# A long convolution beside attention: product stationary and Toeplitz rows streaming in four column tiles, in place of Toeplitz tiles stationary and product streaming

## The chip, the cores and the metric

One core of one Trainium2 chip runs the whole program. The time is microseconds of device time for one execution, and the median of several executions is quoted. All comparisons are between fast runs, and where a single execution is all there is, that is said.

Engines are named as in the profile: PE is the matmul array, PEld its weight loads, DVE the vector engine, ACT the activation engine, POOL and SP the two others. SP does nothing here but issue DMA.

## The reference, cut to what matters

Two independent halves are joined along the last axis. Half A is attention with 32 heads of 16 over 2048 tokens. Half B is a causal convolution of length 2048, one kernel for each of 512 channels. Written as a matrix product, a channel's kernel becomes a Toeplitz matrix: each row is the row above, shifted by one token.

```python
def _A_ref(x, wqkv, wo):                 # x: 1 x 2048 x 512, bf16
    qkv = (x @ wqkv).reshape(B, S, 3, H, Dh)...     # H = 32, Dh = 16
    p = softmax(einsum("bhqd,bhkd->bhqk", q, k) * Dh ** -0.5)
    return einsum("bhqk,bhkd->bhqd", p, v)... @ wo

def _B_ref(q, k, v, shift_k, ssm_k, ssm_D):
    k_shift = sum of k shifted by 0..3 tokens, each times shift_k[:, j]
    kv = k_shift * v                     # the "product", 2048 x 512
    y = causal convolution of kv with ssm_k along the tokens (done there by FFT)
    return q * (y + kv * ssm_D)
```

The attention needs one exp for each of 32 x 2048 x 2048 scores. In this program that is ACT's work alone.

## The kernel before

The program is one long loop of 694 steps. Step T issues up to three score matmuls (row tiles of 32), one exp over what they wrote (128 x 1536), up to three matmuls of an earlier step's probabilities with the values ("PV", column tiles of 32), and one piece of background work on PE: a projection, or one channel of the convolution.

```python
def emit_qk(T): ...      # 3 matmuls, lhsT = KTo[32*s:32*s+32, ...], N = 512, tile_position=(32*s, 0)
                         # then ACT: PT[:, T % R_PT, ...] = exp(SCALE * PS[...])
def emit_pv(bl, T): ...  # 3 matmuls, N = 512, tile_position=(0, 32*s), all into bank PVB

def load_wr(d):          # 128 overlapping rows of channel d's kernel: row p is the kernel shifted by p
    src = bass.AP(tensor=kz_ap.tensor, offset=kz_ap[d, 1].offset, ap=[[1, 128], [1, S]])   # 512 KB
    h_wr[d] = dma(sp, d_wr[r], WR[:, r, :], src, deps)

def conv_chan(d):        # one channel, one step: 16 lags of 128 tokens
    for n in range(NB):                                              # NB = 16
        ins = e.matmul(PS[:, BGB, NB * c + n:NB * c + NB],
                       lhsT=WR[:, r, 128 * n:128 * n + 128],         # Toeplitz tile is stationary
                       rhs=KV[:, 0:NB - n, d], start=(n == 0), stop=(n == NB - 1))  # 16 to 1 columns
    ...                  # after 32 channels DVE multiplies the bank by q
```

The program divides PSUM into eight banks: six alternate between the scores of two steps, one takes PV, one takes the background work (BGB). The exp of step T must be done before the scores of step T+2 may overwrite its banks, so ACT and PE run two steps apart at most.

The softmax here doesn't subtract the row's maximum and nothing guards it: scores larger than these inputs give would overflow.

## Time and profile before

| what | value |
|---|---|
| time | 1153.4 us (1152.6 to 1158.3, 4 runs) |
| profiled execution, span | 1151.7 us |
| start, until the convolution begins | 144 us, 68 steps |
| convolution beside attention | 901 us |
| attention alone, then the end | 90 us + 17 us |

The first view is the page's chart of 40 equal slices, in tenths: how busy PE, ACT and the DMA engines were, and the PE clock that was granted (9 is 90% or more of full speed).

```profile
...
PE   7968999999999999999999999999999999999887
...
ACT  3745898989898989898988898989899889889995
...
PEclk8966855555557565656665656665555575655556
DMA  8742788889997979897989697979999969890000
...
```

PE looks full, ACT is at 80 to 90%, and the DMA engines are at 9 or so in most slices. PEclk: 5 or 6 for nearly the whole convolution stage. PE is "99% busy" (895 of 901 us) at a mean clock of 0.57, mostly 0.50.

Next the costliest groups. After the bar stand busy us and mean ns of one, after the second bar the idle time before them and what ended it.

```profile
...
L387 ACT ACTIVATE PT<-PS 128x1536 bf16<-128x1536 f32 (+1 forms) x694 | 974.4, 1466 | 158.3 <-PE PS L380 156.6
...
L517 PEld LDWEIGHTS PS<-KV,WR 128*128 128x128 bf16 x8192 | 257.5, 103 | 216.4 <-issue 216.4
L517 PE MATMUL PS<-KV,WR 128*128 128x16 bf16 (+15 forms) x8192 | 299.5, 177 | 2.7 <-DVE QT L266 1.8
...
```

ACT waited 157 us for score matmuls, the largest wait that it has; most of it lies between two exps of the convolution stage. PE's convolution shows as 258 us of 128-column weight loads beside matmuls that stream 16 columns or fewer.

The stretches view gives busy time by engine (with the number of instructions), granted clock, DMA share and GB/s for the stage with convolution and for the attention alone after it (an instruction cut by the edge of a stretch counts):

```profile
...
core 0: us, PE busy (x) PEld busy (x) DVE busy (x) ACT busy (x) POOL busy (x), PEclk, DMA share, GB/s
144.00:1045.00 901.00, 894.72 (x11713) 391.96 (x11709) 177.65 (x257) 799.89 (x558) 10.44 (x16) 0.57 0.88 299
1045.00:1135.00 90.00, 78.13 (x407) 14.53 (x404) 16.52 (x24) 90.00 (x68) 0.78 (x1) 0.50 0.03 6
...
```

In the first stage 558 exps fall in 901 us, one in 1.61 us, at a mean clock of 0.57. In the second 68 fall in 90 us, one in 1.33 us, and ACT is busy all the time. So 1.33 us a step is ACT's own floor, and the convolution costs 0.28 us a step above it.

One step of the convolution stage on PE, from the timeline (start, us to the end of the group, what):

```profile
...
602.38 0.62 PE L409 MATMUL PS<-PT,VAF 128*32 128x512 bf16 x3
602.93 0.58 PE L517 MATMUL PS<-KV,WR 128*128 128x16 bf16 x16
603.45 0.61 PE L380 MATMUL PS<-QT,KTo 32*128 32x512 bf16 x3
603.99 0.62 PE L409 MATMUL PS<-PT,VAF 128*32 128x512 bf16 x3
```

Scores to scores takes 1.61 us: scores to PV 0.54, PV to convolution 0.55, convolution 0.52. The convolution's 16 pairs of weight load and matmul follow each other every 27 ns, although no matmul streams more than 16 columns.

### The profile page before, as it was taken

The numbers are of one execution on the slowest core, as the hardware profiler recorded it, in microseconds if no ns is written. First come the engines' busy times: TensorE is split into PE (matmuls) and PEld (weight loads), VectorE is DVE, ScalarE is ACT, GpSimd is POOL, SyncE is SP. The second block draws the span as 40 slices with busy tenths as digits, with TensorE's granted clock in tenths as the row PEclk, the third lists the DMA queues.
The fourth block names the chain that finished last, engine by engine and source line by source line (L and its number), as shares of the span: only waits on it lengthen the run. The fifth ranks groups of instructions, "written<-read, shape, count | busy, mean of one in ns | idle before, by whom it ended". The sixth has DMA issues, their size and how long they took to land.

```text
span 1151.7 us, 27251 instructions
## 1 busy us (share of the span) xinstructions
PE 1102.0 (96%) x12700; PEld 442.1 (38%) x12700; DVE 302.2 (26%) x445; ACT 977.1 (85%) x698; POOL 41.0 (4%) x52
## 2 busy tenths in 40 slices
PE   7968999999999999999999999999999999999887
PEld 2212244444443444444444343444444444442111
DVE  4898412111212011212101212211212111212112
ACT  3745898989898989898988898989899889889995
POOL 4000500000000000000000000000000000000000
PEclk8966855555557565656665656665555575655556
DMA  8742788889997979897989697979999969890000
GB/s 177 257 136 92 237 290 297 291 296 326 323 327 241 331 257 324 272 337 262 334 282 331 224 330 261 329 267 331 339 329 335 326 210 337 292 310 19 1 1 19
DMA packets 98735, 296.03 MB, mean 257 GB/s; under 512 B 18500, under 2 KB 30782, under 8 KB 98494
## 3 DMA queue, kind: packets, MB, share of 16 engines
q1 hardware_dynamic: 94574, 286.16, 74.3%
q0 software_dynamic: 2176, 6.29, 1.9%
q8 instruction: 99, 1.62, 0.6%
q10 hardware_dynamic: 1872, 1.84, 0.6%
q14 instruction: 14, 0.11, 0.0%
HBM read 285.73 MB, written 6.42 MB: 254 GB/s over the span
## 4 chain that ended last, share of the span: by engine, by line
PE 79%; ACT 12%; DVE 7%; DMA 1%; SPq 1%; issue 0%; DVEq 0%
PE PS L409 24%; PE PS L380 24%; PE PS L517 22%; ACT PT L387 12%; PE PS L233 3%; PE PS L472 3%; DVE QT L266 1%; PE PS L252 1%; PE PS L240 1%; DVE OUTA L480 1%; SPq L143 1%; DVE QN L302 1%; DVE DN L432 1%; DMA QN<-in_B_v_dram 1%; DMA xT<-in_A_x_dram 1%; DVE QN L306 1%
## 5 line engine op out<-in xcount | busy, mean ns | idle before, releaser
L387 ACT ACTIVATE PT<-PS 128x1536 bf16<-128x1536 f32 (+1 forms) x694 | 974.4, 1466 | 158.3 <-PE PS L380 156.6
L380 PE MATMUL PS<-QT,KTo 32*128 32x512 bf16 x2048 | 393.2, 561 | 15.9 <-ACT PT L387 13.5
L409 PE MATMUL PS<-PT,VAF 128*32 128x512 bf16 x2048 | 400.6, 567 | 0.0
L517 PEld LDWEIGHTS PS<-KV,WR 128*128 128x128 bf16 x8192 | 257.5, 103 | 216.4 <-issue 216.4
L517 PE MATMUL PS<-KV,WR 128*128 128x16 bf16 (+15 forms) x8192 | 299.5, 177 | 2.7 <-DVE QT L266 1.8
L409 PEld LDWEIGHTS PS<-PT,VAF 128*32 128x32 bf16 x2048 | 74.0, 100 | 273.1 <-issue 261.9
L424 DVE COPY OF<-PS 128x512 f32<-128x512 f32 x32 | 22.1, 692 | 543.1 <-PE PS L409 543.1
L380 PEld LDWEIGHTS PS<-QT,KTo 32*128 32x128 bf16 x2048 | 72.9, 98 | 115.0 <-ACT PT L387 75.2
L432 DVE RECIPROCAL DN<-DN 128x128 f32<-128x128 f32 x128 | 110.7, 916 | 0.9
L528 DVE TENSOR_TENSOR QN<-PS,QN 128x512 bf16<-128x512 f32 x16 | 11.1, 692 | 206.2 <-PE PS L517 206.2
L233 PE MATMUL PS<-xT,WQP 128*128 128x512 bf16 x128 | 43.4, 474 | 6.4 <-DMA xT<-in_A_x_dram 4.7
L472 PE MATMUL PS<-WKV,OTN 128*128 128x512 bf16 x128 | 41.8, 465 | 3.5 <-DVE OTN L437 2.3
L266 DVE CAST QT<-PS 128x512 bf16<-128x512 f32 x32 | 22.1, 691 | 33.4 <-PE PS L233 33.4
L426 DVE STREAM_SHUFFLE DN<-OF 128x512 f32<-128x512 f32 x32 | 24.1, 754 | 0.0
L143 POOL DMA_DIRECT2D out_dram<-QN x4 | 4.7, 1173 | 539.2 <-DVE QN L528 539.2
L437 DVE TENSOR_TENSOR OTN<-OF,DN 128x512 bf16<-128x512 f32 (+1 forms) x35 | 22.6, 646 | 1.2
L233 PEld LDWEIGHTS PS<-xT,WQP 128*128 128x128 bf16 x128 | 11.4, 110 | 29.7 <-issue 9.1
L472 PEld LDWEIGHTS PS<-WKV,OTN 128*128 128x128 bf16 x128 | 12.1, 111 | 27.2 <-issue 13.2
L240 PE MATMUL PS<-xT,WKV 128*128 128x512 bf16 x64 | 20.9, 459 | 0.9 <-DVE KTo L270 0.9
L252 PE MATMUL PS<-WKV,xT 128*128 128x512 bf16 x64 | 18.3, 413 | 2.7 <-DVE VAF L280 2.7
L245 PE MATMUL PS<-KV,JEX 128*128 128x512 bf16 x16 | 7.9, 491 | 13.0 <-DVE KV L310 10.8
L143 POOL DMA_DIRECT2D out_dram<-OUTA x12 | 6.5, 544 | 353.5 <-DVE OUTA L480 353.5
(39 smaller groups left out, 151.3 us busy)
## 6 DMA issues: line engine op xcount, KB each, us to landing
WR<-kz_scratch SPq DMA_DIRECT2D x512, 512.0 KB, 6.0
WR<-in_B_k_dram SPq DMA_DIRECT2D x16, 256.0 KB, 3.8
QN<-in_B_k_dram SPq DMA_DIRECT2D x13, 256.0 KB, 3.6
kz_scratch<-WR SPq DMA_DIRECT2D x1, 2176.0 KB, 7.9
WR<-in_B_ssm_k_dram SPq DMA_DIRECT2D x1, 2048.0 KB, 9.2
QN<-in_B_q_dram POOLq DMA_DIRECT2D x16, 128.0 KB, 2.6
out_dram<-QN POOLq DMA_DIRECT2D x4, 512.0 KB, 7.3
out_dram<-OUTA POOLq DMA_DIRECT2D x12, 128.0 KB, 2.0
```

Source lines behind the costliest of these rows:

```text
L143: f(outp, inp).then_inc(dsem.sem, 16)
L233: return e.matmul(PS[:, bank, :], lhsT=WQP[:, dc, g, :], rhs=xT[:, dc, qb * 512:(qb + 1) * 512], start=(dc == 0), stop=(dc == 3))
L240: return e.matmul(PS[:, bank, :], lhsT=WK[:, dc, o * 128:(o + 1) * 128], rhs=xT[:, dc, sc * 512:(sc + 1) * 512], start=(dc == 0), stop=(dc ...
L252: return e.matmul(PS[:, bank, :], lhsT=xT[:, dc, kt * 128:(kt + 1) * 128], rhs=WV[:, dc, :], start=(dc == 0), stop=(dc == 3))
L266: hh = dve.op(lambda e: e.tensor_copy(QT[:, qb % 2, g, :], PS[:, bank, :]), [h])
L380: ins = e.matmul(PS[:, bank, :], lhsT=KTo[32 * s:32 * s + 32, g // 2, kt * 128:(kt + 1) * 128], rhs=QT[32 * s:32 * s + 32, qb % 2, g, :], ...
L387: h_exp[T] = act.op(lambda e: e.activation(PT[:, T % R_PT, 0:n * QB], PS[:, banks[0]:banks[0] + n, :].rearrange("p b f -> p (b f)"), ACT.E ...
L409: ins = e.matmul(PS[32 * s:32 * s + 32, PVB, :], lhsT=VAF[:, kt, h * VW:h * VW + 32], rhs=PT[:, Tc % R_PT, j * QB:(j + 1) * QB], start=(kt ...
L426: h_sh = dve.op(lambda e: e.stream_shuffle(out=DN[:, r, :], in_=OF[:, r, :], mask=[DH] * 32), [h_of, h_otn.get(n - 2)])
L432: rec[i] = dve.op(lambda e: e.reciprocal(DN[:, r, sl], DN[:, r, sl]), [h_sh])
L472: ins = e.matmul(PS[:, bank, :], lhsT=OTN[:, qb % 2, g, t * 128:(t + 1) * 128], rhs=WOP[:, g, :], start=(g == 0), stop=(g == NG - 1))
L517: ins = e.matmul(PS[:, BGB, NB * c + n:NB * c + NB], lhsT=WR[:, r, 128 * n:128 * n + 128], rhs=KV[:, 0:NB - n, d], start=(n == 0), stop=(n ...
```

## The change

The intent is to turn the convolution's operands round. The product is stationary, at most 16 columns, and 128 columns of the Toeplitz rows stream. Four channels run at once in the four column tiles of 32. The output is then transposed and time-reversed, so the kernel is stored reversed, the product's tiles are stored in reverse order, and eight transposes for each 32 channels turn the result back. The channel count per step is the same: a step does 4 of 16 lags for four channels. The core of the diff:

```diff
-R_W = 8
-R_PT = 5
+R_W = 12
+R_PT = 4
+R_O = 11
-N_EARLY = 66
+N_EARLY = 44
+LAGS = 4
...
-    def conv_chan(d):
...
-            for n in range(NB):
-                ins = e.matmul(PS[:, BGB, NB * c + n:NB * c + NB],
-                               lhsT=WR[:, r, 128 * n:128 * n + 128],
-                               rhs=KV[:, 0:NB - n, d], start=(n == 0), stop=(n == NB - 1))
+    def conv_lags(qd, n0, n1):
...
+            for n in range(n0, n1):
+                for c in range(4):
+                    d = 4 * qd + c
+                    ins = e.matmul(PS[32 * c:32 * c + NB - n, BGB, 128 * (kk % 4):128 * (kk % 4) + 128],
+                                   lhsT=KV[:, n:NB, d],
+                                   rhs=WR[:, d % R_W, 128 * (NB - 1 - n):128 * (NB - n)],
+                                   start=(n == 0), stop=(n == NB - 1), tile_position=(0, 32 * c))
...
+    def conv_turn(b):          # after 32 channels: 8 transposes, then DVE multiplies by q
...
+            ho = dma(pool, d_outB[sl % 2], dst, QN[:, sl % 2, :, :], [hh])
+            if sl + 2 < 4:
+                load_qn(sl + 2, [ho])
```

To make room, the q slices are loaded in four parts through two buffers (`load_qn`) and the attention outputs go through a ring of 11. The 16 matmuls that reversed the product are gone. Loads of k and v move from SP's to POOL's queue, and POOL also writes the reversed kernel and rearranges the taps.

More of the change, by code (lines that the diff above doesn't have):

```diff
@@ L110, in bass_concat_heads__mha_block__ssm_conv_h3__prompt_kernel @@
     KV = sb("KV", [128, NB, C])
-    QN = sb("QN", [128, NB, C])
+    QN = sb("QN", [128, 2, NB, 128])
     WQP = sb("WQP", [128, 4, NG, 128])
     WKV = sb("WKV", [128, 2, 4, D])
-    OTN = sb("OTN", [128, 2, NG, QB])
+    OTN = sb("OTN", [128, R_O, QB])
     OF = sb("OF", [128, 2, QB], FP32)
@@ L117, in bass_concat_heads__mha_block__ssm_conv_h3__prompt_kernel @@
     OUTA = sb("OUTA", [128, 2, D])
-    JEX = sb("JEX", [128, 128])
+    YB = sb("YB", [128, 2, 512])
+    IDN = sb("IDN", [128, 128])
     JNK = sb("JNK", [128, 2], FP32)
@@ L122, in bass_concat_heads__mha_block__ssm_conv_h3__prompt_kernel @@
     WOP = WKV[:, :, :, :].rearrange("p a c f -> p (a c) f")
-    WST = OTN[:, 0, 0:4, :]
+    WST = OTN[:, 7:11, :]
     wr_flat = WR[:, :, :].rearrange("p r w -> p (r w)")
-    qn_flat = QN[:, :, :].rearrange("p t d -> p (t d)")
     KZS = wr_flat[:, 0:4 * LKZ].rearrange("p (c m) -> p c m", c=4)
-    TRAW = wr_flat[:, 4 * LKZ:4 * LKZ + 2048].rearrange("p (d m) -> p d m", m=4)
-    o1 = 4 * LKZ + 2048
-    kvbuf = [qn_flat[:, 0:5120].rearrange("p (m t d) -> p m t d", m=5, t=2),
-             wr_flat[:, o1:o1 + 5120].rearrange("p (m t d) -> p m t d", m=5, t=2)]
-    TB = qn_flat[:, 5120:5120 + 2048].rearrange("p (m d) -> p m d", m=4)
-    DSS = qn_flat[:, 7680:7684].rearrange("p (c m) -> p c m", m=1)
+    DSS = wr_flat[:, 4 * LKZ:4 * LKZ + 4].rearrange("p (c m) -> p c m", m=1)
+    o1 = 5 * S
+    kvbuf = [wr_flat[:, o1 + 5120 * i:o1 + 5120 * i + 5120].rearrange("p (m t d) -> p m t d", m=5, t=2)
+             for i in range(2)]
+    TRAW = wr_flat[:, o1 + 10240:o1 + 12288].rearrange("p (d m) -> p d m", m=4)
+    TB = wr_flat[:, o1 + 12288:o1 + 14336].rearrange("p (m d) -> p m d", m=4)
+    KZN = [QT[:, 1, :, :].rearrange("p g f -> p (g f)").rearrange("p (c s) -> p c s", c=2),
+           QN[:, :, :, :].rearrange("p b t d -> p (b t d)").rearrange("p (c s) -> p c s", c=2)]
     PS = enter(nc.psum_tensor("PS", [128, 8, 512], FP32))
@@ L149, in bass_concat_heads__mha_block__ssm_conv_h3__prompt_kernel @@
     d_kv = [DmaSem(sem(f"d_kv{i}")) for i in range(8)]
-    d_tap, d_kz, d_kzw, d_q, d_wo, d_outB = [DmaSem(sem(n)) for n in
-                                             ("d_tap", "d_kz", "d_kzw", "d_q", "d_wo", "d_outB")]
+    d_tap, d_kz, d_kzw, d_wo = [DmaSem(sem(n)) for n in ("d_tap", "d_kz", "d_kzw", "d_wo")]
+    d_q = [DmaSem(sem(f"d_q{i}")) for i in range(2)]
+    d_outB = [DmaSem(sem(f"d_outB{i}")) for i in range(2)]
     d_outE = DmaSem(sem("d_outE"))
@@ L159, in bass_concat_heads__mha_block__ssm_conv_h3__prompt_kernel @@
     h_wk = dma(act, d_w[1], WK, wview[:, :, D:2 * D])
-    h_wv = dma(act, d_w[2], WV, wview[:, :, 2 * D:3 * D])
+    h_traw = dma(act, d_tap, TRAW, bass.AP(tensor=B_shift_k.tensor, offset=B_shift_k[0, 0].offset,
+                                          ap=[[0, 128], [4, C], [1, 4]]))
     h_x = [None] * 4
@@ L177, in load_kv @@
             if j == 0 and m > 0:
-                dma(sp, d_kv[j], b[m:128, m, 0, :], k2[0:128 - m, :], deps)
+                dma(pool, d_kv[j], b[m:128, m, 0, :], k2[0:128 - m, :], deps)
                 src = bass.AP(tensor=kap.tensor, offset=k2[128 - m, 0].offset, ap=[[D, 128], [1, D]])
-                dma(sp, d_kv[j], b[:, m, 1, :], src, deps)
+                dma(pool, d_kv[j], b[:, m, 1, :], src, deps)
             else:
@@ L183, in load_kv @@
                               ap=[[D, 128], [128 * D, 2], [1, D]])
-                dma(sp, d_kv[j], b[:, m, :, :], src, deps)
-        h_kv[j] = dma(sp, d_kv[j], b[:, 4, :, :], vap, deps)
+                dma(pool, d_kv[j], b[:, m, :, :], src, deps)
+        h_kv[j] = dma(pool, d_kv[j], b[:, 4, :, :], vap, deps)
     h_j = dve.op(lambda e: e.memset(JNK[:], 0.0))
@@ L190, in bass_concat_heads__mha_block__ssm_conv_h3__prompt_kernel @@
     h_wq0 = dve.op(lambda e: e.memset(WQP[:, :, 0:2, :], 0.0))
-    h_j0 = pool.op(lambda e: e.memset(JEX[:, :], 0.0))
-    h_jex = pool.op(lambda e: e.affine_select(out=JEX[:, :], in_=JEX[:, :], compare_op=ALU.not_equal, fill=1.0,
-                                              base=-127, pattern=[[1, 128]], channel_multiplier=1), [h_j0])
-    h_vaf1 = pool.op(lambda e: e.memset(VAF[:, :, :], 1.0))
+    h_wq1 = dve.op(lambda e: e.memset(WQP[:, :, 2:8, :], 0.0))
+    vones = VAF[:, :, 0:H * VW].rearrange("p k (h e) -> p k h e", e=VW)
+    pool.op(lambda e: e.memset(vones[:, :, :, DH:VW], 1.0))
+    h_vaf1 = pool.op(lambda e: e.memset(VAF[:, :, H * VW:VROW], 1.0))
     h_kvz = pool.op(lambda e: e.memset(kvbuf[0][0:3, 1:4, 0, :], 0.0))
-    h_kz0 = pool.op(lambda e: e.memset(KZS[:, :, 0:PAD], 0.0))
-    h_wq1 = pool.op(lambda e: e.memset(WQP[:, :, 2:8, :], 0.0))
+    load_kv(0, h_kvz)
+    load_kv(1)
+    h_kz0 = pool.op(lambda e: e.memset(KZS[:, :, S:S + PAD], 0.0))
+    h_id0 = pool.op(lambda e: e.memset(IDN[:, :], 0.0))
+    h_idn = pool.op(lambda e: e.affine_select(out=IDN[:, :], in_=IDN[:, :], compare_op=ALU.not_equal, fill=1.0,
+                                              base=0, pattern=[[-1, 128]], channel_multiplier=1), [h_id0])
     act.op(lambda e: e.activation(JNK[:, 1:2], JNK[:, 0:1], ACT.Exp), [h_j], inc=False)
     load_x(0)
+    h_wv = dma(sp, d_w[2], WV, wview[:, :, 2 * D:3 * D])
     load_x(1)
-    h_traw = dma(sp, d_tap, TRAW, bass.AP(tensor=B_shift_k.tensor, offset=B_shift_k[0, 0].offset,
-                                          ap=[[0, 128], [4, C], [1, 4]]))
-    load_kv(0, h_kvz)
+    kzview = B_ssm_k.rearrange("(p c) s -> p c s", c=4)
+    for i in range(2):
+        dma(sp, d_kz, KZN[i], kzview[:, 2 * i:2 * i + 2, :])
+    h_kzl = dma(sp, d_kz, DSS, B_ssm_D.rearrange("(p c m) -> p c m", c=4, m=1))
     load_x(2)
     load_x(3)
-    load_kv(1)
-    dma(sp, d_kz, KZS[:, :, PAD:PAD + S], B_ssm_k.rearrange("(p c) s -> p c s", c=4))
-    h_kzl = dma(sp, d_kz, DSS, B_ssm_D.rearrange("(p c m) -> p c m", c=4, m=1))
     h_wqp = {}
@@ L241, in mm @@
                                 rhs=xT[:, dc, sc * 512:(sc + 1) * 512], start=(dc == 0), stop=(dc == 3))
-        elif kind == "r":
-            _, t, hp = u
-            deps += [hp, h_jex]
-            return pe.op(lambda e: e.matmul(PS[:, bank, :], lhsT=JEX[:, :], rhs=KV[:, t, :], start=True, stop=True),
-                         deps)
         else:
@@ L265, in evac_unit @@
             _, qb, g = u
-            hh = dve.op(lambda e: e.tensor_copy(QT[:, qb % 2, g, :], PS[:, bank, :]), [h])
+            hh = dve.op(lambda e: e.tensor_copy(QT[:, qb % 2, g, :], PS[:, bank, :]), [h, h_kzt[0] if qb == 1 else None])
             h_q[(qb, g)] = hh
@@ L271, in evac_unit @@
             h_k[(o, sc)] = hh
-        elif kind == "r":
-            _, t, hp = u
-            hh = dve.op(lambda e: e.tensor_copy(KV[:, t, :], PS[:, bank, :]), [h])
-            h_kvc[0] = hh
         else:
@@ L288, in bass_concat_heads__mha_block__ssm_conv_h3__prompt_kernel @@
     kv_pieces = []
-    revs = []
     h_kvc = [None]
-    h_tb = [None]
-    def kv_piece_tb():
-        h_tb[0] = dve.op(lambda e: e.tensor_copy(TB.rearrange("p m d -> p d m"), TRAW), [h_traw])
+    h_tb = [pool.op(lambda e: e.tensor_copy(TB.rearrange("p m d -> p d m"), TRAW), [h_traw])]
     def kv_chunk(j):
@@ L309, in last @@
         def last():
-            h = dve.op(lambda e: e.tensor_tensor(KV[:, 2 * j:2 * j + 2, :], b[:, 3, :, :], b[:, 4, :, :], ALU.mult), [st["a"]])
+            for i in range(2):
+                h = dve.op(lambda e, i=i: e.tensor_tensor(KV[:, NB - 1 - 2 * j - i, :], b[:, 3, i, :], b[:, 4, i, :],
+                                                          ALU.mult), [st["a"]])
             h_kvfree[j] = h
-            revs.append((2 * j, h))
-            revs.append((2 * j + 1, h))
+            h_kvc[0] = h
             if j + 2 < 8:
@@ L320, in bass_concat_heads__mha_block__ssm_conv_h3__prompt_kernel @@
     h_kzw = [None]
-    h_kzd = pool.op(lambda e: e.tensor_tensor(KZS[:, :, PAD:PAD + 1], KZS[:, :, PAD:PAD + 1], DSS, ALU.add),
-                    [h_kzl, h_kz0])
-    h_kzw[0] = dma(sp, d_kzw, kz_ap.rearrange("(p c) m -> p c m", c=4), KZS, [h_kzd])
+    h = None
+    for c in range(4):
+        rev = KZN[c // 2][:, c % 2, :]
+        rev = bass.AP(tensor=rev.tensor, offset=KZN[c // 2][:, c % 2, S - 1:S].offset, ap=[rev.ap[0], [-1, S]])
+        h = pool.op(lambda e, c=c, rev=rev: e.tensor_copy(KZS[:, c, 0:S], rev), [h_kzl])
+    h_kzt = [h]
+    h = pool.op(lambda e: e.tensor_tensor(KZS[:, :, S - 1:S], KZS[:, :, S - 1:S], DSS, ALU.add), [h])
+    h_kzw[0] = dma(sp, d_kzw, kz_ap.rearrange("(p c) m -> p c m", c=4), KZS, [h, h_kz0])
     for o in range(1, 4):
         kv_pieces.append(lambda o=o: emit_wqp(o))
-    kv_pieces.append(kv_piece_tb)
     for j in range(8):
@@ L394, in bass_concat_heads__mha_block__ssm_conv_h3__prompt_kernel, with oslot @@
     h_pvb = [None]
+    def oslot(n):
+        return (n + 6) % R_O
     h_otn = {}
@@ L436, in mult @@
             h_otn[(n, i1)] = h_otn[n] = dve.op(
-                lambda e: e.tensor_tensor(OTN[:, qb % 2, g, sl], OF[:, r, sl], DN[:, r, sl], ALU.mult),
-                [rec[i1 - 1]] + [h_op.get((qb - 2, t)) for t in range(4)] + [h_wqp[7]])
+                lambda e: e.tensor_tensor(OTN[:, oslot(n), sl], OF[:, r, sl], DN[:, r, sl], ALU.mult),
+                [rec[i1 - 1], h_wqp[7]] + ([h_op[((n - R_O) // NG, t)] for t in range(4)] if n >= R_O else []))
         if last:
@@ L471, in fn @@
             for g in range(g0, g1):
-                ins = e.matmul(PS[:, bank, :], lhsT=OTN[:, qb % 2, g, t * 128:(t + 1) * 128], rhs=WOP[:, g, :],
+                ins = e.matmul(PS[:, bank, :], lhsT=OTN[:, oslot(qb * NG + g), t * 128:(t + 1) * 128], rhs=WOP[:, g, :],
                                start=(g == 0), stop=(g == NG - 1))
@@ L493, in op_out_end, with load_qn @@
         dma(act if t % 2 else sp, d_outE, out2[r0:r0 + 128, 0:D], dst, [hh])
-    h_conv = {}
-    h_wr = {}
-    h_qn = [None]
-    h_ybank = [None]
+    h_wr, h_wrfree, h_qn = {}, {}, {}
+    h_yb = [None]
     def load_wr(d):
         r = d % R_W
-        deps = [h_kzw[0], h_kvc[0]] if d < R_W else [h_conv[d - R_W]]
-        src = bass.AP(tensor=kz_ap.tensor, offset=kz_ap[d, 1].offset, ap=[[1, 128], [1, S]])
+        deps = [h_kzw[0], h_kvc[0]] if d < R_W else [h_wrfree[d - R_W]]
+        src = bass.AP(tensor=kz_ap.tensor, offset=kz_ap[d, 0].offset, ap=[[1, 128], [1, S]])
         h_wr[d] = dma(sp, d_wr[r], WR[:, r, :], src, deps)
-    def conv_chan(d):
-        c = d % CHB
-        r = d % R_W
-        deps = [h_wr[d], h_kvc[0]]
-        if c == 0:
+    def load_qn(i, deps):
+        h_qn[i] = dma(pool, d_q[i % 2], QN[:, i % 2, :, :],
+                      q2[:, 128 * i:128 * i + 128].rearrange("(t p) d -> p t d", p=128), deps)
+    def conv_lags(qd, n0, n1):
+        kk = qd % 8
+        deps = [h_wr[4 * qd + c] for c in range(4)] + [h_kvc[0]]
+        if kk % 4 == 0 and n0 == 0:
             deps.append(bank_free[BGB])
@@ L515, in fn @@
             ins = None
-            for n in range(NB):
-                ins = e.matmul(PS[:, BGB, NB * c + n:NB * c + NB],
-                               lhsT=WR[:, r, 128 * n:128 * n + 128],
-                               rhs=KV[:, 0:NB - n, d], start=(n == 0), stop=(n == NB - 1))
-            return ins
-        h_conv[d] = pe.op(fn, deps)
-        if d + R_W < C:
-            load_wr(d + R_W)
-        if c == CHB - 1:
-            b = d // CHB
-            yv = PS[:, BGB, :].rearrange("p (c t) -> p t c", c=CHB)
-            qv = QN[:, :, CHB * b:CHB * b + CHB]
-            h = dve.op(lambda e: e.tensor_tensor(qv, yv, qv, ALU.mult), [h_conv[d], h_qn[0]])
-            bank_free[BGB] = h
-            if b % 4 == 3:
-                B4 = b // 4
-                dst = out2[:, D + 128 * B4:D + 128 * (B4 + 1)].rearrange("(t p) c -> p t c", p=128)
-                dma(pool, d_outB, dst, QN[:, :, 128 * B4:128 * (B4 + 1)], [h])
+            for n in range(n0, n1):
+                for c in range(4):
+                    d = 4 * qd + c
[3 more added lines that the diff above has]
+                                   start=(n == 0), stop=(n == NB - 1), tile_position=(0, 32 * c))
@@ new lines, in fn @@
+            return ins
+        h = pe.op(fn, deps)
+        if n1 == NB:
+            for c in range(4):
+                h_wrfree[4 * qd + c] = h
+                if 4 * qd + c + R_W < C:
+                    load_wr(4 * qd + c + R_W)
+            if kk % 4 == 3:
+                half = kk // 4
+                src = PS[:, BGB, :]
+                src = bass.AP(tensor=src.tensor, offset=PS[:, BGB, 127:128].offset,
+                              ap=[src.ap[0], [128, 4], [-1, 128]])
+                hh = dve.op(lambda e: e.tensor_copy(YB[:, half, :].rearrange("p (k i) -> p k i", k=4), src),
+                            [h, h_yb[0]])
+                bank_free[BGB] = hh
@@ new lines, in conv_lags, with fn @@
+        return h
+    def conv_turn(b):
+        pbf = PS[:, BGB, :].bitcast(BF16)
+        def fn(e):
+            ins = None
+            for k in range(8):
+                ins = e.transpose(pbf[:, 128 * k:128 * k + 128], YB[:, k // 4, 128 * (k % 4):128 * (k % 4) + 128],
+                                  IDN[:, :])
+            return ins
+        h = pe.op(fn, [bank_free[BGB], h_idn])
+        h_yb[0] = h
+        sl = b // 4
+        yv = pbf.rearrange("p (c j) -> p c j", j=32)[:, :, 0:NB].rearrange("p c j -> p j c")
+        yv = bass.AP(tensor=yv.tensor, offset=pbf[:, NB - 1:NB].offset, ap=[yv.ap[0], [-1, NB], [32, CHB]])
+        qv = QN[:, sl % 2, :, CHB * (b % 4):CHB * (b % 4) + CHB]
+        hh = dve.op(lambda e: e.tensor_tensor(qv, yv, qv, ALU.mult), [h, h_qn[sl]])
+        bank_free[BGB] = hh
+        if b % 4 == 3:
+            dst = out2[:, D + 128 * sl:D + 128 * (sl + 1)].rearrange("(t p) c -> p t c", p=128)
+            ho = dma(pool, d_outB[sl % 2], dst, QN[:, sl % 2, :, :], [hh])
+            if sl + 2 < 4:
+                load_qn(sl + 2, [ho])
@@ L542, in bass_concat_heads__mha_block__ssm_conv_h3__prompt_kernel @@
     later_op = [(qb, t) for qb in range(NQB - 1) for t in range(4)]
-    state = {"early": 0, "chan": 0, "q": 0, "op": 0, "half": None, "gap": 0, "rev": 0}
+    state = {"early": 0, "qd": 0, "lag": 0, "turn": False, "q": 0, "op": 0, "half": None, "gap": 0, "started": False}
     def emit_bg(T):
         st = state
-        bank = (5, 7)[T % 2] if T < N_EARLY - 2 else 7
-        if revs and (T % 2 == 0 or st["early"] == len(early)):
-            unit(("r",) + revs.pop(0), bank)
-            st["rev"] += 1
-            return
         if st["early"] < len(early):
-            unit(early[st["early"]], bank)
+            unit(early[st["early"]], (5, 7)[T % 2] if T < N_EARLY - 2 else 7)
             st["early"] += 1
@@ L557, in emit_bg @@
             return
+        if not kv_pieces and not st["started"]:
+            st["started"] = True
+            for d in range(R_W):
+                load_wr(d)
+            for i in range(2):
+                load_qn(i, [h_kvc[0], h_kzt[0]])
+            return
+        if st["turn"]:
+            conv_turn(st["qd"] // 8 - 1)
+            st["turn"] = False
+            st["gap"] = 0
+            return
         if st["half"] is not None:
             qb, t = st["half"]
-            h = op_mm(qb, t, 4, 8, BGB)
-            op_out(qb, t, BGB, h)
+            op_out(qb, t, BGB, op_mm(qb, t, 4, 8, BGB))
             st["half"] = None
             return
-        boundary = st["chan"] % CHB == 0 and st["rev"] == NB
-        if boundary and st["gap"] < 3:
-            st["gap"] += 1
+        if st["qd"] % 8 == 0 and st["lag"] == 0:
             if st["op"] < len(later_op):
                 qb, t = later_op[st["op"]]
-                if T >= (qb + 1) * 171 + 10 and (qb * NG + NG - 1) in h_otn:
+                if (qb * NG + NG - 1) in h_otn:
                     op_mm(qb, t, 0, 4, BGB)
@@ L573, in emit_bg @@
                     return
-            if st["q"] < len(later_q):
+            if st["gap"] < 3 and st["q"] < len(later_q):
                 u = later_q[st["q"]]
                 if u[1] < 2 or T >= (u[1] - 1) * 171:
+                    st["gap"] += 1
                     unit(u, BGB)
@@ L579, in emit_bg @@
                     return
-        if st["chan"] < C and st["rev"] == NB and T >= N_EARLY + 2:
-            if st["chan"] == 0:
-                if not h_wr:
-                    for d in range(R_W):
-                        load_wr(d)
-                    for t in range(NB):
-                        h_qn[0] = dma(pool, d_q, QN[:, t, :], q2[t * 128:(t + 1) * 128, :], [h_kvc[0]])
-            conv_chan(st["chan"])
-            st["chan"] += 1
-            st["gap"] = 0
+        if st["started"] and st["qd"] < C // 4:
+            n0 = st["lag"]
+            n1 = min(n0 + LAGS, NB)
+            conv_lags(st["qd"], n0, n1)
+            st["lag"] = n1 % NB
+            if n1 == NB:
+                st["qd"] += 1
+                st["turn"] = st["qd"] % 8 == 0
     def pe_last():
@@ L620, in bass_concat_heads__mha_block__ssm_conv_h3__prompt_kernel @@
                 item[1]()
-        for _ in range(1 if T < 22 else 2):
+        for _ in range(1 if T < 38 else 2):
             if kv_pieces and T >= 1:
                 kv_pieces.pop(0)()
-    assert state["chan"] == C and state["q"] == len(later_q) and state["op"] == len(later_op), state
+    assert state["qd"] == C // 4 and not state["turn"] and state["q"] == len(later_q) and state["op"] == len(later_op), state
     assert not dve_later and not kv_pieces
@@ L634, in bass_concat_heads__mha_block__ssm_conv_h3__prompt_kernel @@
         op_out_end(qb, t, banks[t], h)
-    for ds in (d_outA[0], d_outA[1], d_outB, d_outE):
+    for ds in (d_outA[0], d_outA[1], d_outB[0], d_outB[1], d_outE):
         sp.op(lambda e, ds=ds: e.wait_ge(ds.sem, ds.n), inc=False)
```

## The prediction

> **What bounds the kernel now.** The stretches view shows three stages. Until 144 us (68 of 694 steps) DVE is busiest. From 144 to about 1045 us the convolution runs with attention: exps start 1.607 us apart while one takes 1.450 us, and the waits view has ACT waiting for scores matmuls (157 us): PE bounds it. The timeline divides a step at half clock (PEclk 0.50): scores 0.54 us, PV 0.55 us, one channel of convolution (16 pairs of 128-column weight load and matmul with 16 to 1 columns, 27 ns apart) 0.52 us. In the tail (from 1045 us, no convolution) the exps follow each other every 1.330 us: that is ACT's floor.
>
> **What the change does to a step.** Each step now takes 4 lags of 4 channels: 16 matmuls with 128 moving columns in four column tiles. A PV burst with five matmuls in the trace (297.08 us) shows such tiles: four start within 10 ns, and the fifth, in the tile of the first, starts 402 ns later with its weights already loaded. [...] Estimate at half clock: 4 x 107 (a quarter of 427 ns, the spacing of 512 columns) = 0.43 us; PV to convolution needs no tile-mode change (the 0.11 us that scores and PV pay). Step: 0.54 + 0.43 + 0.43 + 0.11 = 1.51 us.
>
> **Clock.** By streamed columns, a half-clock 3.4 us stretch of this trace is followed by full clock where it streams 83% or more (358 us: 87%), not at 75% or less; the old step streams 60 to 63%. The new one streams 1.28/1.51 = 85%. At full clock PE needs about 0.85 us a step, so ACT bounds at 1.33 us, streaming 48%; full-clock stretches fell back at 42% or less. I expect mostly full clock with relapses, 1.36 us a step (1.33 to 1.42).
>
> **DMA.** Unchanged, 512 KB for each channel, now 394 GB/s during convolution steps, about 350 over all slots. A burst at 124 to 130 us moved 418 GB/s, the loads landing 1.29 us apart. It nearly binds.
>
> **Rest.** 16 reversal matmuls and their DVE casts (11 us) go, the 5.4 us tap copy leaves DVE, convolution starts at step 55, not 68. Added: 16 transposes x 8, 32 reversing PSUM copies of about 0.69 us, reversed copies and KV loads on POOL, which may stall DVE for about 10 us. Convolution starts at about 118 us (estimate).
>
> **Sum.** 118 + 576 slots x 1.36 (783) + about 59 tail steps x 1.33 (78) + 17 at the end = 996; I say 1000 us, range 965 to 1070 (the top: 1.51 us steps throughout). Chances: faster 0.95, within 2% 0.03, slower 0.02.
>
> **What would show it.** Right: in the convolution stage PEclk well over 0.6, ACT busy near 97% and exps 1.33 us apart, no PE wait for row loads, convolution 0.25 to 0.45 us. Clock step wrong: PEclk 0.50 and 1.51 us a step. DMA step wrong: PE waits for row loads, DMA share 1.0, step 1.4 us or more. Tiling step wrong: convolution matmuls of one tile more than 107 ns apart, step over 1.6 us.
>
> **What would make it wrong.** Weight loads that don't overlap in a column tile; the clock counting 16-column matmuls as little activity; PE waiting for DVE's reversing copies.

One sentence is cut above, which gave a rule for weight loads that no run here shows. No term of the sum rested on it: 118 + 783 + 78 + 17 = 996, as recorded. The other figures of a step can be read from the trace before. Scores to PV take 0.54 us at half clock, where 512 columns take 0.43: that is the 0.11 us (at full clock 0.32 and 0.22). That PV to convolution pays none was a forecast; the trace after shows 0.01 us between their starts. The 0.85 us a step at full clock is an estimate that adds up from these: 0.32 + 2 x 0.21 (half of 0.43) + 0.11. That DVE can stall beside POOL is seen there too: two copies of 128x256 (L219), at 4.93 and 5.08 us, took 4.5 us each and ended at 9.5 us, with POOL's memset of 9472 columns (1.4 to 9.4 us); six later ones, with POOL idle, took 0.22 us each. The 10 us for it are the author's estimate, against 4.6 us in the trace after.

## The result, and the profile after

| | before | after |
|---|---|---|
| median | 1153.4 us | 1031.8 us (1029.7 to 1032.6, 4 runs) |
| ratio of fast runs | | 0.8935, 95% interval 0.8907 to 0.8962 |
| span of the profiled execution | 1151.7 us | 1029.9 us |
| mean granted clock | 0.60 | 0.92 |

A ratio is the mean time of one kernel's fast runs over that of the other's fast runs of the same rounds, so it is not quite the ratio of the medians quoted.

The same four rows of the page's chart:

```profile
...
PE   4998267777766877777677876777767686767887
...
ACT  1678379999997899999999999999999999999995
...
PEclk7999589999999999999998999999999999996556
DMA  9723599899997498999999769898999959970000
...
```

PE is no longer full. The clock and ACT are at 9 in nearly every slice of the convolution stage (from the sixth to the 36th). DMA is where it was. The groups:

```profile
...
L388 ACT ACTIVATE PT<-PS 128x1536 bf16<-128x1536 f32 (+1 forms) x690 | 933.1, 1642 | 79.3 <-PE PS L381 79.0
...
L525 PE MATMUL PS<-WR,KV 128*16 128x128 bf16 (+15 forms) x8192 | 309.7, 225 | 22.9 <-DMA WR<-kz_scratch 19.4
...
```

There are as many convolution matmuls as before (8192), and each streams 128 columns where it was 16 to 1. ACT's mean duration went up from 1466 to 1642 ns while its work is the same. When there is nothing to wait for, the records overlap: near 1060 us in the trace before, exps recorded at 1.6 us start 1.33 us apart. So a recorded duration includes time behind the predecessor. The distance between starts is the measure, and that is 1.33 us when ACT is full.

```profile
...
core 0: us, PE busy (x) PEld busy (x) DVE busy (x) ACT busy (x) POOL busy (x), PEclk, DMA share, GB/s
139.00:936.00 797.00, 587.44 (x11857) 298.45 (x11866) 205.33 (x297) 778.10 (x572) 13.54 (x18) 0.98 0.90 338
936.00:1016.00 80.00, 69.21 (x357) 13.04 (x356) 11.72 (x17) 80.00 (x60) 0.00 (x0) 0.50 0.00 1
...
```

With the convolution, 572 exps start in 797 us (1.39 us each) at clock 0.98. In the tail without it the clock falls to 0.50 and the exps still come every 1.34 us: there PE has so little to do (69 of 80 us busy) that half speed is enough.

A step on PE, scores to scores, at full clock:

```profile
...
312.57 0.39 PE L381 MATMUL PS<-QT,KTo 32*128 32x512 bf16 x3 [0.49 <-ACT PT L388]
312.89 0.40 PE L414 MATMUL PS<-PT,VAF 128*32 128x512 bf16 x3
312.90 0.61 PE L525 MATMUL PS<-WR,KV 128*12 128x128 bf16 x16
313.94 0.39 PE L381 MATMUL PS<-QT,KTo 32*128 32x512 bf16 x3 [0.43 <-ACT PT L388]
```

PE needs 0.32 us for the scores. Then PV and the convolution start 0.01 us apart, because three PV matmuls leave one column tile free and the channel in that tile starts at once. In the single records of this step its four matmuls start at 312.90 to 313.11 us, and those of the other three tiles from 313.12 us, although the program issues the four tiles in turn for each lag. PE then waits for ACT, which the bracket on the last line says. At half clock before, scores (row tiles) to PV (column tiles) took 0.54 us where 512 columns alone take 0.43 (the spacing of the projections' matmuls): the change of tiles cost 0.11 us. Here PV to convolution (both column tiles) starts after 0.01 us and costs nothing of the kind.

The waits view:

```profile
...
PEld PS L381 <- ACT PT L388: 333.3, 585, 0.9
...
ACT PT L388 <- PE PS L381: 79.0, 77, 17.9
...
PE PS L525 <- DMA WR<-kz_scratch: 19.4, 6, 14.3
...
```

It is now PE that waits for ACT. ACT's wait for scores has halved to 79 us, most of it in the start and in a few gaps that are explained below. PE waited for row loads in six places, 19 us in all.

### The profile page after: what moved, and what is told of

Its sections match the earlier page's. It is cut to its first block, busy times and chain, and to the rows that moved or that the text cites. A ratio compares the mean times of both kernels' runs of the same rounds, so it can differ in the third digit from the quotient of the medians.

```text
span 1029.9 us, 27703 instructions
## 1 busy us (share of the span) xinstructions
PE 760.0 (74%) x12790; PEld 343.5 (33%) x12812; DVE 310.7 (30%) x469; ACT 935.8 (91%) x694; POOL 75.8 (7%) x88
## 4 chain that ended last, share of the span: by engine, by line
ACT 75%; PE 9%; DVE 6%; DMA 6%; POOL 1%; SPq 1%; issue 1%; DVEq 0%
ACT PT L388 75%; DMA WR<-kz_scratch 3%; PE PS L477 2%; PE PS L242 2%; PE PS L381 2%; DMA WKV<-in_A_wqkv_dram 2%; PE PS L414 1%; PE PS L256 1%; DVE WR L298 1%; SPq L147 1%; DVE QT L270 1%; DMA out_dram<-QN 1%; DVE WR L302 1%; DVE DN L437 1%; PE PS L249 1%
## 5 line engine op out<-in xcount | busy, mean ns | idle before, releaser
L388 ACT ACTIVATE PT<-PS 128x1536 bf16<-128x1536 f32 (+1 forms) x690 | 933.1, 1642 | 79.3 <-PE PS L381 79.0
L381 PE MATMUL PS<-QT,KTo 32*128 32x512 bf16 x2048 | 288.6, 412 | 203.3 <-ACT PT L388 199.9
L525 PE MATMUL PS<-WR,KV 128*16 128x128 bf16 (+15 forms) x8192 | 309.7, 225 | 22.9 <-DMA WR<-kz_scratch 19.4
L414 PE MATMUL PS<-PT,VAF 128*32 128x512 bf16 x2048 | 293.7, 416 | 7.9 <-DVE OF L429 7.9
L525 PEld LDWEIGHTS PS<-WR,KV 128*14 128x14 bf16 (+15 forms) x8192 | 207.2, 106 | 46.2 <-issue 31.4
L541 DVE CAST YB<-PS 128x512 bf16<-128x512 f32 x32 | 22.1, 691 | 317.0 <-PE PS L525 317.0
L242 PE MATMUL PS<-xT,WQP 128*128 128x512 bf16 x119 | 32.2, 389 | 14.8 <-DMA xT<-in_A_x_dram 10.3
L477 PE MATMUL PS<-WKV,OTN 128*128 128x512 bf16 x121 | 33.4, 403 | 11.4 <-DVE OUTA L485 5.7
L147 POOL DMA_DIRECT2D WR<-in_B_k_dram x35 | 24.3, 699 | 34.7 <-DVE KV L307 34.4
L298 DVE TENSOR_TENSOR WR<-WR 128x1024 bf16<-128x1024 bf16 x32 | 24.9, 787 | 5.2 <-DMA WR<-in_B_v_dram 5.2
```

Of the source, the lines that this page charges most:

```text
L147: f(outp, inp).then_inc(dsem.sem, 16)
L242: return e.matmul(PS[:, bank, :], lhsT=WQP[:, dc, g, :], rhs=xT[:, dc, qb * 512:(qb + 1) * 512], start=(dc == 0), stop=(dc == 3))
L298: st[m] = dve.op(lambda e: e.tensor_tensor(b[:, m, :, :], b[:, m, :, :], in1, ALU.mult), [h_kv[j], h_tb[0]])
L381: ins = e.matmul(PS[:, bank, :], lhsT=KTo[32 * s:32 * s + 32, g // 2, kt * 128:(kt + 1) * 128], rhs=QT[32 * s:32 * s + 32, qb % 2, g, :], ...
L388: h_exp[T] = act.op(lambda e: e.activation(PT[:, T % R_PT, 0:n * QB], PS[:, banks[0]:banks[0] + n, :].rearrange("p b f -> p (b f)"), ACT.E ...
L414: ins = e.matmul(PS[32 * s:32 * s + 32, PVB, :], lhsT=VAF[:, kt, h * VW:h * VW + 32], rhs=PT[:, Tc % R_PT, j * QB:(j + 1) * QB], start=(kt ...
```

## The experiments

Below, the share that a stretch streams is worked out from the trace: the time in which at least one matmul's columns (columns over granted clock, counted from its start) run, in each of the 3.4 us intervals in which the clock record changes (its stretches in the traces before and after are multiples of 3.41 us, at 0.50 or 1.00). Of columns, 512 took 216 ns at full clock and 426 at half in the trace before. Some matmul records can be missing from a trace, so a share can be a few per cent low.

The theory after the result: **the clock**. PE's clock goes to full when matmuls stream columns for most of the time, and falls to half below some share. This is read from the traces: in the trace before, most of the half-clock stretches of the convolution stage stream 58 to 63% and stay at half, while those of 83% or more (with projections) are followed by full clock, and the last full-clock stretches before a fall stream 42% or less. The old convolution spends its time on pairs of weight load and matmul 27 ns apart and streams 7 ns of them on average (8.5 columns at half clock), so half clock is granted and PE bounds. The new one streams, so the clock rises and ACT bounds. The rival: **the shorter block**. Four channels at once and one change of tiles less (0.11 us) make PE's step shorter, and the clock is a by-product.

The trace after gives one hint by itself. Near 540 us the clock fell to half for some steps:

```profile
...
540.08 0.61 PE L381 MATMUL PS<-QT,KTo 32*128 32x512 bf16 x3
540.62 0.61 PE L414 MATMUL PS<-PT,VAF 128*32 128x512 bf16 x3
540.63 1.03 PE L525 MATMUL PS<-WR,KV 128*4 128x128 bf16 x16
541.59 0.61 PE L381 MATMUL PS<-QT,KTo 32*128 32x512 bf16 x3
...
```

Scores to scores is 1.51 us there. So at half clock the change would have taken 0.10 us off a step of 1.61, and the rest of the way to 1.33 is the clock's.

One thing must be said about correctness. The check of the whole output doesn't see the convolution half well, because with the reference's inputs its values are small beside the attention's: three runs below whose convolution is wrong on purpose (before_wide64, before_wide24, half_rows) were called correct (tiles2 and tiles1, wrong on purpose too, were called wrong). So "correct" says little about the convolution of an experiment; where a result is called right here, that of the change included, it is by construction of the edit.

### 1. The old convolution with more columns (before_wide64)

```diff
-                ins = e.matmul(PS[:, BGB, NB * c + n:NB * c + NB],
+                ins = e.matmul(PS[:, BGB, min(NB * c, 448):min(NB * c, 448) + 64],
                                lhsT=WR[:, r, 128 * n:128 * n + 128],
-                               rhs=KV[:, 0:NB - n, d], start=(n == 0), stop=(n == NB - 1))
+                               rhs=KV[:, n, 0:64], start=True, stop=True)
```

> The kernel before with one edit: every convolution matmul streams 64 columns in place of 16 to 1, so the convolution streams 7.5 times more columns (wrong result on purpose). Clock theory (the change pays because more streamed columns bring the full clock; the old order would be as fast at full clock): at half clock the step would be 0.54+0.55+0.85+0.11 = 2.0 us with 84% streamed, so the clock goes to full and stays (64% streamed there); exps 1.33 to 1.40 us apart in the convolution stage, PEclk above 0.85, 1153 - 565 x 0.23 = about 1020 us (1010 to 1060). Rival (the change pays because its convolution block and mode switches are shorter): more streamed columns cost time, 1153 us or more, PEclk near 0.6.

Measured: 1014.1 us (1012.3 to 1014.5, 4 runs), ratio to the kernel before 0.8802 (0.8775 to 0.8829). The stage with convolution:

```profile
...
core 0: us, PE busy (x) PEld busy (x) DVE busy (x) ACT busy (x) POOL busy (x), PEclk, DMA share, GB/s
144.00:930.00 786.00, 749.80 (x11812) 395.15 (x11824) 182.20 (x265) 777.88 (x577) 11.22 (x16) 0.98 0.90 343
...
```

The old order with 7.5 times more columns is 12% faster than the old order, and faster than the change. 577 exps start in 786 us (1.36 us) at clock 0.98. The pairs are 29 ns apart at full clock, against 27 in the old kernel at either clock, so the extra columns cost 2 ns a pair. Whether the weight load or the issue of a matmul sets the 27 ns, no run here separates. The rival falls: neither column tiles nor fewer mode changes are needed, a full clock is enough. The edit also gave each matmul its own accumulation; experiment 3 has that too and takes 1.62 us a step while its clock is at half, so it is not what pays. This kernel computes a wrong convolution and is no candidate.

### 2. The change with two column tiles, and with one (tiles2, tiles1)

```diff
-                    ins = e.matmul(PS[32 * c:32 * c + NB - n, BGB, ...
+                    j = c % 2        # tiles1: c % 1
+                    ins = e.matmul(PS[32 * j:32 * j + NB - n, BGB, ...
-                                   start=(n == 0), stop=(n == NB - 1), tile_position=(0, 32 * c))
+                                   start=True, stop=True, tile_position=(0, 32 * j))
```

> The changed kernel with the four channels in two column tiles instead of four (wrong result on purpose, each matmul its own accumulation). Clock theory: at full clock PE needs 0.32+0.21+8x0.053+0.11 = 1.07 us a step, still under the 1.33 us of ACT, so the time stays within 1.5% of the changed kernel's 1031 us, PEclk above 0.9. Rival (four concurrent channels are what pays): 8 x 53 ns = 0.2 us more in each of 512 steps, about 1140 us.

> The changed kernel with all four channels in one column tile (wrong result on purpose). Clock theory: full clock (PEclk above 0.9), but PE needs 0.32+0.21+16x0.053+0.11 = 1.50 us a step, more than ACT's 1.33, so PE bounds again and 512 steps cost 0.15 us more: about 1110 us (1090 to 1160). If the matmuls of one tile are more than 53 ns apart (weight loads not hidden), more[...].

Measured: two tiles 1028.9 us (4 runs, ratio 0.8925, 0.8894 to 0.8956), the same as the change's 0.8935. One tile 1123.0 us (one run). Two tiles, then one:

```profile
...
core 0: us, PE busy (x) PEld busy (x) DVE busy (x) ACT busy (x) POOL busy (x), PEclk, DMA share, GB/s
139.00:936.00 797.00, 692.83 (x11882) 382.32 (x11892) 204.40 (x297) 777.60 (x576) 13.55 (x18) 0.99 0.90 339
...
```

```profile
...
core 0: us, PE busy (x) PEld busy (x) DVE busy (x) ACT busy (x) POOL busy (x), PEclk, DMA share, GB/s
139.00:1030.00 891.00, 865.60 (x11909) 576.70 (x11920) 203.90 (x297) 819.88 (x577) 13.54 (x18) 0.99 0.86 303
...
```

Halving the concurrency costs nothing: 576 exps in the same 797 us, PE busier, ACT still the limit. Taking it away altogether leaves the clock at 0.99 and makes PE the limit again: 577 exps in 891 us, 1.54 us each, where 1.50 was expected. The matmuls of the one tile followed each other every 56 ns in the trace; its timeline has 16 of them in 1.08 us:

```profile
...
401.28 1.08 PE L526 MATMUL PS<-WR,KV 128*16 128x128 bf16 x16
...
```

At full clock 128 columns alone take 54 ns (a quarter of the 216 ns between 512-column matmuls of the projections), so new weights of 16 columns or fewer for each matmul added 2 ns: the loads were hidden. So the tiles do have a part: swapped operands on one tile would have given 1123 us. Two are enough.

### 3. A little more streaming in the old order (before_wide24)

The edit is that of experiment 1 with 24 columns in place of 64 (wrong result).

> The kernel before with every convolution matmul streaming 24 columns (wrong result on purpose): 2.8 times more columns than before, but at half clock they stay hidden behind the 27 ns between pairs, and a step streams (0.85+0.32)/1.61 = 73%. Clock theory: below the 81 to 83% that brought the full clock in the trace before, so PEclk stays at about 0.6 and the time at 1140 to 1165 us. Rival (any column more helps, or it was the separate accumulations that made the 64-column kernel fast): 1100 us or less.

Measured: 1115.7 us (one run), mean clock 0.69. Not what was expected, and the trace shows why. The whole stage, then two neighbouring stretches:

```profile
...
core 0: us, PE busy (x) PEld busy (x) DVE busy (x) ACT busy (x) POOL busy (x), PEclk, DMA share, GB/s
144.00:1045.00 901.00, 872.00 (x11891) 386.56 (x11888) 183.95 (x269) 823.65 (x587) 11.25 (x16) 0.68 0.86 299
410.00:431.00 21.00, 19.60 (x295) 9.47 (x294) 7.57 (x11) 19.36 (x15) 0.54 (x1) 0.98 0.71 244
431.00:460.00 29.00, 28.99 (x395) 12.79 (x396) 5.50 (x8) 26.50 (x19) 0.00 (x0) 0.50 0.99 346
...
```

At half clock the kernel behaved as expected (1.62 us a step; its 3.4 us stretches mostly stream for 69 to 75% of the time, and stayed at half clock). But after each group of projections, which bring the full clock (in the trace before, the half-clock stretch ahead of the change streams 80 to 90% there), it held the full clock longer, because at full clock it streams 40 to 53% and the old kernel about 42%. From 410 to 431 us the clock was 0.98 and 15 exps fell in the 21 us (1.40 us each). Then it fell to half. So the share at which the clock rose and the share at which it fell are two, and I had looked at the upper one alone. In the trace before, half-clock stretches of 75% or less stayed at half and all of 83% or more went to full. Full-clock stretches of 42% were sometimes the last ones there, and such of 43 and 44% in the trace after. As measured over all kept traces but the slow one, neither limit is sharp: between 68 and 83% a half-clock stretch was followed by either clock and from 84% always by full clock; full-clock stretches up to 44% were sometimes the last, those of 45% or more never.

### 4. Is DMA at its limit? (half_rows, ring8)

half_rows loads half of each Toeplitz row after the first 12 (wrong result). ring8 uses eight of the twelve row buffers.

```diff
 half_rows:
-        h_wr[d] = dma(sp, d_wr[r], WR[:, r, :], src, deps)               # src rows of S elements
+        h_wr[d] = dma(sp, d_wr[r], WR[:, r, 0:S // 2], src, deps)        # src rows of S // 2, for d >= R_W
 ring8:
-        r = d % R_W
+        r = d % RING                                                     # RING = 8, at all uses
```

> The changed kernel with each Toeplitz row load cut to half its bytes after the first 12 (wrong result on purpose). If the loads nearly bind in the convolution stage: the waits for row loads after 200 us vanish, the step's median goes from 1.34 to 1.330 us, and about 10 to 25 us of the changed kernel's 1031 us go. If DMA has slack: within 5 us of it, with the stalls near 320 and 543 us unchanged.

> The changed kernel with the row buffers used as a ring of 8 in place of 12. The rows of a quad are then asked for one quad ahead (4 steps, 5.3 us) but take 7.3 us or more to land four of them. Expected if the buffers' depth carries the change: each quad lasts 7.3 us, 1.83 us a step, about 1270 us, with PE waiting for row loads and relapses of the clock. If depth matters little: under 1050 us.

Measured: half_rows 1026.1 us (2 runs, ratio 0.8912, 0.8873 to 0.8951: not distinguishable from the change's 0.8935 at this precision; the 5.7 us lie between the two expectations, nearer to that of slack). In its trace the gap of 3.2 us near 553 us, where PE had waited for a row load, is gone; the 8.5 us gap near 328 us shrank to 6.4; the typical distance between exps stayed at 1.33 us.

```profile
...
core 0: us, PE busy (x) PEld busy (x) DVE busy (x) ACT busy (x) POOL busy (x), PEclk, DMA share, GB/s
139.00:936.00 797.00, 584.41 (x11875) 297.14 (x11886) 206.41 (x297) 782.11 (x576) 13.58 (x18) 0.99 0.59 175
...
```

Half the bytes (175 GB/s in place of 338) buy about the same number of exps in the same 797 us. The loads don't bound the stage. ring8 took 1212.4 us (one run, mean clock 0.80), slower than the kernel before, with PE waiting 73 times:

```profile
...
PE PS L526 <- DMA WR<-kz_scratch: 214.5, 73, 15.4
...
```

So with twelve buffers the bytes don't bound the stage, and with eight the loads lack time ahead; eight buffers with fewer bytes were not tried. Rows are freed and asked for four at a time (the four channels that run at once, a quad), and a load took 7.8 us from issue to landing in the changed kernel (median), more than the 5.3 us of one quad's four steps. The expectation of 1270 us was too high, the direction right.

### 5. Where the remaining time went (early_rows, late_qn)

Two gaps between exps stand out in the trace after: 15.8 us at 117 us, and 8.5 us at 328 us. The chain of waits names what released the steps around the first (start, us, what):

```profile
...
101.20 4.74 DMA WR<-in_B_v_dram
...
122.50 16.21 DMA WR<-kz_scratch
...
```

The row buffers also hold the product chunks and the kernel matrix during the start, so the first row loads wait for the last chunk. Twelve loads are then issued at once, together with the first q slices. The second gap, on POOL's queue and on DVE:

```profile
...
319.24 1.17 POOL L147 DMA_DIRECT2D out_dram<-QN  x1 [197.91 <-DVE QN L561]
327.88 1.15 POOL L147 DMA_DIRECT2D QN<-in_B_q_dram  x1 [7.47 <-DMA out_dram<-QN]
329.02 1.11 POOL L147 DMA_DIRECT2D out_dram<-OUTA  x2
...
```

```profile
...
333.90 0.69 DVE L485 CAST OUTA<-PS 128x512 bf16<-128x512 f32 x1 [8.36 <-DMA out_dram<-OUTA]
```

POOL stores a finished q slice (512 KB), then its queue stands for 7.5 us until that store has landed, because the next command, the reload of the same buffer, waits for it. Two attention outputs queue up behind. Their buffers stay taken, so the next copy out of PSUM waits 8.4 us on DVE, and PE waits for that bank. This wait is new; the kernel before loaded all of q once.

```diff
 early_rows:
+        if d < 5:    deps = [h_kzw[0]]                 # issued before the loop
+        elif d < 7:  deps = [h_kzw[0], h_kvfree[6]]    # issued with the last but one chunk
+        else:        deps = ...as before
 late_qn:
-            if sl + 2 < 4:
-                load_qn(sl + 2, [ho])
+            h_ob[sl] = ho
+        if b in (4, 8):                                # one turn (32 channels) later
+            load_qn(sl + 1, [h_ob[sl - 1]])
```

> The changed kernel with the first seven row loads issued as soon as their place is free (five after the kernel matrix is in DRAM, two after the last but one product chunk) in place of after the last chunk. Theory: the 15.8 us gap between exps at 117 us is the wait for the first four rows; it falls to 4 us or less and the time to 1031 - 13 = 1018 us. Rival (the gap is made up elsewhere, since DMA or DVE bound the start): 1028 us or more.

> The changed kernel with the reload of the q slices issued one turn later, so that POOL's queue doesn't stand waiting for the 512 KB store while the attention's stores queue behind it. Theory: the 8.5 us gap between exps at 328 us goes (to 2.2 us or less), the time falls by 6 to 10 us to about 1023 us. Rival (the store itself or the DMA load makes the gap): gap stays, 1029 us or more.

Measured: late_qn 1025.4 us (4 runs, ratio 0.8891, 0.8866 to 0.8916). The gap fell from 8.5 to 2.2 us and POOL no longer stands before the outputs:

```profile
...
320.48 1.17 POOL L147 DMA_DIRECT2D out_dram<-QN  x1 [198.11 <-DVE QN L562]
323.84 0.56 POOL L147 DMA_DIRECT2D out_dram<-OUTA  x1 [2.19 <-DVE OUTA L485]
...
335.04 1.17 POOL L147 DMA_DIRECT2D QN<-in_B_q_dram  x1 [0.17 <-issue]
```

early_rows 1025.2 us (4 runs, ratio 0.8886, 0.8860 to 0.8913). Its gap fell from 15.8 to 2.9 us as expected, but only half of that was gained: eight steps later a new gap of 6.3 us appeared, because the rows of the third quad were still in the queue (the last of the first twelve landed at 134 us). The first rows had come early; the burst behind them hadn't. The second gap also grew, from 8.5 to 10.0 us. The intervals of both touch that of the change (0.8907 to 0.8962), so each gain is small; that the named gaps closed is seen in the traces.

### 6. Together (best1, best2)

best1 has both edits, loads the output weights after the product chunks, puts the load of the value weights back on ACT's queue and loads the second chunk after the tap copy. best2 adds two more moves of loads.

```diff
 best1 (beside the two edits above):
-                load_wop(pe_last())       # when the early projections end
+            load_wop(pe_last())           # when the product is done
-    h_wv = dma(sp, ...)                   # after the first x tiles
+    h_wv = dma(act, ...)                  # third on ACT's queue
-    load_kv(0, h_kvz); load_kv(1)
+    load_kv(0, h_kvz)                     # load_kv(1) after the tap copy
 best2 (beside best1):
+    q slices first loaded at the fourth quad; load_kv(0) waits for the first x tiles
```

> The changed kernel with both edits above, the output weights loaded after the product chunks, the value weights back on ACT's queue ahead of the taps, and the second product chunk loaded after the tap copy. Expected: 13 + 8 us from the two waits, 5 us from the chunk that waited behind the output weights, about 5 us at the start: 1000 us (990 to 1012).

> The combined kernel with the q slices first loaded twelve steps after the convolution begins, out of the way of the rows of quads 1 and 2, and the first product chunk loaded after the first x tiles. Expected: the 9.4 us gap at 125 us falls to 3 us or less, first exp at 18 us in place of 23.5: 1017 - 6 - 4 = about 1007 us.

Measured: best1 1017.6 us (1014.3 to 1022.1, 4 runs), ratio to the kernel before 0.8833 (0.8798 to 0.8869), the best kernel here with a right result, and apart from the change's interval. I had hoped for 1000: a gap of 9.4 us at 125 us remained, again the third quad's rows. best2 was a miss: 1023.2 us (ratio 0.8897, 0.8871 to 0.8922). Its gap was still 8.6 us. My edit moved the place of the q load in POOL's program, but no wait ties POOL to that step, so it ran ahead and issued the load at 128 us all the same, into the same burst. The first exp did come earlier (18.8 us in place of 23.6), but the chunks came later, and step 20 was reached at 64.8 us in place of 56.9.

### 7. The old order at full clock with a right result (before_wide, before_wide_ct)

If streaming is all that the old kernel lacks, it can stream the columns of eight channels where one is needed. The seven others fall into PSUM columns that their own channel's first matmul overwrites later.

```diff
 before_wide:
+                k = min(CHB - c, 8)
+                yw = PS[:, BGB, :].rearrange("p (c t) -> p t c", c=CHB)[:, n:NB, c:c + k]
-                ins = e.matmul(PS[:, BGB, NB * c + n:NB * c + NB], lhsT=WR[...], rhs=KV[:, 0:NB - n, d], ...)
+                ins = e.matmul(yw, lhsT=WR[...], rhs=KV[:, 0:NB - n, d:d + k], ...)
 before_wide_ct, beside that, the product stored with the tokens innermost, and yw and rhs taken channel by channel:
-    KV = sb("KV", [128, NB, C])
+    KV = sb("KV", [128, C * NB])[:, :].rearrange("p (d t) -> p t d", t=NB)
```

> The kernel before with a right result: every convolution matmul streams the columns of up to eight channels in place of one (the other seven fall in columns that their own channel overwrites later), 8 x (16 - n) columns, 68 on average. Clock theory: as fast as the 64-column experiment, 1010 to 1035 us, so faster than the changed kernel's 1031 or equal to it, PEclk above 0.85, exps 1.33 us apart. Rival (the time of the 64-column experiment came from its separate accumulations or its lost dependences): 1100 us or more.

> The widened kernel before (eight channels per matmul, right result) with the product stored channel by channel, so that the moving operand and the PSUM columns run in stretches of 16 - n neighbours and not in strides of 1 KB and 64 bytes. If the strides made its matmuls slow[...], it reaches the time of the 64-column experiment, 1010 to 1035 us. If the widening with eight channels is slow for another reason, 1120 us or more again, at a clock above 0.9.

Measured: before_wide 1174.7 us (median of five fast runs; ratio 1.0183, 1.0154 to 1.0211: slower than before, though by less than 2%), although those runs had a clock of 0.93 to 0.94. That is far from the 1010 to 1035 us of the clock theory, and the number that the rival had named; what answers the rival is the next run, which keeps the accumulations and the dependences. A full clock alone is therefore not the whole rule: PE must also get through its step in 1.33 us. Its profile fell in the slow state (1432 us at a mean clock of 0.64), so I read no spacing from it. before_wide_ct took 1064.9 us (4 runs, ratio 0.9260, 0.9226 to 0.9294). Its stage with convolution:

```profile
...
core 0: us, PE busy (x) PEld busy (x) DVE busy (x) ACT busy (x) POOL busy (x), PEclk, DMA share, GB/s
196.00:950.00 754.00, 739.98 (x11605) 433.09 (x11604) 176.01 (x256) 744.37 (x552) 10.08 (x15) 1.00 0.93 356
...
```

There 552 exps start in 754 us, 1.37 us each at clock 1.00: nearly ACT's floor, with a right result in the old order. The whole time misses the 1010 to 1035 us expected, because of the start (below). So the strides were what made the first version slow; whether those on the reading side or those on the PSUM side isn't settled, as the edit changed both: the operand had been read in runs of 16 bytes with a step of 1 KB, and the output had stepped by 64 bytes. No run here separates the two. The new layout costs elsewhere: the convolution began at step 68 at 191.6 us and not at 143.7, in a start whose product chunks DVE now writes with a stride. What takes the time there I did not measure.

## Why the prediction was right or wrong

- **What bounds the kernel before: right.** PE at half clock, with ACT's floor at 1.33 us. Shown by experiment 1.
- **The step at half clock, 1.51 us: right.** The steps at 540 us show 1.51.
- **Tiling, with weight loads hidden in a column tile: right.** 56 ns between matmuls in one tile at full clock (tiles1), where 128 columns alone take 54. Four tiles are more than needed (tiles2).
- **The clock: right in its outcome.** 0.98 in the stage, exps at 1.33 to 1.35 us. "Mostly full with relapses" is what the trace shows. The upper limit held for the change (half-clock stretches of the trace after that streamed 74% or less stayed at half, those followed by full clock streamed 78 to 89%); the lower was slightly low: three relapses of the stage followed stretches of 43 to 44%, where the prediction had 42% or less. Experiment 3, made with the upper one alone, went wrong.
- **DMA "nearly binds": too cautious.** Half the bytes gave about the same time. But the sign that the prediction named for its right case, no PE wait for row loads, did not come: PE waited six times, 19 us in all, 14.3 of them before the first convolution step. What the twelve buffers give is time ahead (ring8).
- **The sum: 996 us against a span of 1029.9.** The terms, from the start of the exps in the trace: the convolution stage began with a step at 133 us and not at 118 (+15); 576 slots took 803 us and not 783 (+20); the tail 80 and not 78; the end 14 and not 17. The prediction gave the first term as an estimate without its parts (that I had about 8 us in mind for the first rows' landing is not on record). What it missed: twelve rows and two q slices landed together and the exps stood for 15.8 us; experiment early_rows closed that gap and showed the next one behind it. The second was mis-sized by gaps: those of more than 1.73 us after the start add up to about 21 us above the floor, the largest of them 8.5 us on POOL's queue, which late_qn removed. That a queue would stand behind its own store was not in the prediction at all.
- **DVE stalls early "about 10 us": seen in part.** While POOL copied the reversed kernel (32 to 41 us), four DVE multiplications and additions took 1.8 to 2.0 us in place of 0.68, 4.6 us in all, and DVE waited 5.2 us once at 101 us for a chunk queued behind the output weights on POOL.

## What to carry to other kernels

Read the granted clock before anything else in a kernel whose PE looks full: PE at 99% busy was PE at a mean clock of 0.57 here, and work that streamed more columns, even useless ones, made the whole kernel faster (1014 us in place of 1153, before_wide64). A change of operands is worth what it does to the engine that then bounds (here ACT at 1.33 us a step), so going from one tile to two paid (1123 to 1029 us) and from two to four paid nothing (1032). When you reuse buffers through a store and a reload, don't put the reload straight behind the store on a queue that others use (POOL's stood for 7.5 us here); and remember that moving a command in a queue's program moved nothing in time where nothing made that queue wait (best2: the q load went out at 128 us all the same).
